# The last 64 keys of two neighbouring batches as one chunk, and the sums of two key chunks in one visit

## The chip, the cores and the metric

The kernel runs on one core of a Trainium2 chip. The core has five engines that work side by side, each with its own queue in order: TensorE (PE, the matrix unit; loads of its stationary operand are shown apart as PEld), VectorE (DVE), ScalarE (ACT), GpSimd (POOL) and SyncE (SP, which issues the DMAs here). SBUF holds tiles of 128 partitions; PE writes into PSUM, 8 banks of 512 float32 per partition. The metric is the device time of one execution in microseconds (us), as the median of several runs.

## The reference

Random-feature attention over 8 batches of 8 heads, 576 positions, 64 values per head, 128 features, then a layer norm and a two-layer MLP with a residual:

```python
def phi(x):
    proj = np.einsum('bhsd,md->bhsm', x, omega)
    sq = np.sum(x * x, axis=-1, keepdims=True) / 2.0
    h = proj - sq
    h = h - np.max(h, axis=-1, keepdims=True)
    return np.exp(h) / np.sqrt(m)
q_p, k_p = (phi(q_s), phi(k_s))
kv = np.einsum('bhsm,bhsd->bhmd', k_p, v)
z = np.sum(k_p, axis=2)
num = np.einsum('bhsm,bhmd->bhsd', q_p, kv)
den = np.einsum('bhsm,bhm->bhs', q_p, z)[..., None] + 1e-06
return (num / den).astype(np.float32)
...
xn = (x - mu) / np.sqrt(var + 1e-06) * g_ln
ch = np.maximum(xn @ w_ch1, 0.0) @ w_ch2
return (x + ch).astype(np.float32)
```

Here x is the attention's output, [batch, position, 8 heads x 64]; w_ch1 is 512 x 2048, w_ch2 2048 x 512.

## The kernel before

**MLP, the stream on PE.** The 8 x 576 = 4608 rows are 9 tiles (t) of 512 rows. For each tile mm1 (L723) computes 16 blocks (f) of 128 hidden features, and mm2 (L759) adds each block into four result banks. Every product is split into three matmuls on high and low parts (L737 to L739, L770 to L772), 3456 in all with 512 columns each. The input xnT is the normalised x, transposed on PE (L710, four 128x128 transposes for each of the 36 row chunks of 128) and split by ACT (L714) and DVE (L716). Weights (w1, w2; 32 loads of 512 KB) are unpacked and split once by ACT and DVE (gen_w, L363 to L434), some ten steps for each.

**Attention.** A batch's 576 keys are five chunks: four of 128 (NFULL) and one of 64 (REM). For each chunk gen_k (L456) loads keys and values (L460, L461), projects the keys (L518, 8 matmuls that the trace shows as 16 records), takes the maximum on DVE (L521) and the exponential on ACT (L527, 8 of them) into a tile kp, and then forms the sums (L491): for each head two matmuls of 64 features x 65 columns (64 values and a one, so that z comes along), 16 matmuls or 32 records. After each chunk of batches 1 to 7 the sums are added into the tile kv by DVE (L504; the first is copied, L507); batch 0's five chunks add up in PSUM instead (banks 6 and 7) and are copied once. The queries go by 36 chunks of 128 rows (gen_q, L535): the first 8 are projected in fp32 (L550), the others in split matmuls (L568, L569); then a copy out of PSUM (L573), a maximum over partitions on POOL (L580), DVE's difference (L585) and ACT's exponential (L588). gen_x (L611) forms numerators and denominators with kv (L627, a visit of 32 records), divides (L634 to L638) and takes the row's statistics (L655, L657).

**What sets the order.** All of this is written by generators, which a planner (class Plan, L68) runs through a model of engines, latencies and free places; the order in which it lets them go on is the order of the program. The steps on PE that interrupt the MLP's stream are called visits below. A part with a lower rank goes first; one that holds PSUM banks is moved ahead by 100 (L57). Once the MLP runs, all visits share one pair of PSUM banks (b_at, banks 0 and 1), mm1 has two banks and mm2 four; before that every pair is free to use, except banks 6 and 7 for batch 0's sums. VISIT (0.37 us) is what the planner adds to a visit's cost. While PE would stand idle in the start, gen_warm (L796) sets in small bf16 matmuls ("spin", L336).

**Places.** "wide" tiles (4) take raw keys and queries and serve weight steps; v (3 places), kp (2), kv (3) and quad (5) serve the attention. In the start, batch 0's loads may also use the weight tiles that are filled last: n_first names them, two for each of FIRST = 4 f (L288). kTr and vR hold the 64-key chunks: kTr is [batch, 128, 4, 64], vR [batch, 64, 8, 65].

Of the kernel before, what the change touches and what calls it, by code (L numbers as in the profile page):

```python
# [16 lines left out]
AF = mybir.ActivationFunctionType  # L17
# [187 lines left out]
def favor_ffn(ctx, tc, kT, kTr, vF, vR, qT, qD, omT, gT, w1, w2, out):  # L205
# [93 lines left out]
    def at_now():  # L299
        return b_at if mlp_on else banks  # L300

    def pairs_now():
        return (b_at,) if mlp_on else tuple(banks[i : i + 2] for i in range(0, 8, 2))

# [131 lines left out]
    kvs, phis, xs, xnTs, pvs, pvt = {}, {}, {}, {}, {}, {}  # L436


    def gen_keys():
        for b in range(B):  # L440
            if b == 1:
                yield wait("w", 2, GATE_K)
            t_kv = yield "get", n_kv
            kvs[b] = t_kv, heads_of(t_kv)
            for c in range(NFULL + 1):
                plan.cur.rank = NS * (b * S // T) + RK + 2 * c
                r = P if c < NFULL else REM
                first = n_first if b == 0 else ()
                k_turn = () if first else ((yield "get", turn["k"]),)
                t_k = yield "get", first + n_big  # L450
                kraw = tile_of(t_k, [P, NP, r])
                t_v = yield "get", first + n_v
                v = heads_of(t_v)
                plan.add(plan.cur.rank, gen_k(b, c, r, kraw, v, (t_k, *k_turn), t_v, n_kp + first))

    def gen_k(b, c, r, kraw, v, early, t_v, n_kp):  # L456
        rank = plan.cur.rank
        kv = kvs[b][1]
        yield dma(2 * P * NP * r)
        nc.sync.dma_start(kraw, kT[b, c] if c < NFULL else kTr[b])  # L460
        nc.sync.dma_start(v[0:r], vF[b, c] if c < NFULL else vR[b])  # L461
        if c:
            yield wait("k", b, c - 1)
        t_kp = yield "get", n_kp
        t_mb = yield "get", n_mb
        late = t_kp, t_mb, t_v
        done(("k", b, c))
        kp = tile_of(late[0], [P, H, M])
        mb = tile_of(late[1], [P, H])
        yield wait("om")  # L470

        def values():
            yield us(DVE, 0.08)
            nc.vector.memset(v[0:r, :, D : D + 1], 1.0)
            done(("v", b, c))

        def sums():
            yield wait("v", b, c)
            yield wait("kp", b, c)
            if c:  # L480
                yield wait("kvmm", b, c - 1)
            if b:
                pvs[0] = yield "pair", pairs_now()
            elif c == 0:
                pvs[0] = banks[6:8]
            t_b = pvs[0]
            yield "run", {PE: VISIT + 0.94}, 0.03
            pv = two(t_b, 4 * (D + 1)).rearrange("p s (a b) -> p s a b", b=D + 1)
            for h in range(H):
                for a in (0, D):  # L490
                    nc.tensor.matmul(  # L491
                        pv[a : a + D, h // 4, h % 4], kp[0:r, slot(h), a : a + D], v[0:r, h],
                        start=(b > 0 or c + h % 4 == 0), stop=(b > 0 or (c == NFULL and h % 4 == 3)),
                    )
            done(("kvmm", b, c))
            free(*late)
            if b == 0 and c < NFULL:
                return
            o = kv.rearrange("p (s a) b -> p s (a b)", s=2)
            pv = two(t_b, 4 * (D + 1))  # L500
            if b and c:
                yield wait("kv", b, c - 1)
                yield dve(8 * (D + 1))
                nc.vector.tensor_tensor(out=o, in0=pv, in1=o, op=ALU.add)  # L504
            else:
                eng = yield "run", {ACT: 0.53, DVE: 0.61}
                copy(eng, o, pv)  # L507
            free(*t_b)
            done(("kv", b, c))

        plan.add(rank, values())
        t_b = yield "pair", pairs_now()
        yield "run", {PE: VISIT + 0.95}, 0.03
        pk = two(t_b).rearrange("p s (a b) -> p s a b", b=M)
        for p in range(NP):
            for h in range(2):
                a = slice(h * D, (h + 1) * D)
                nc.tensor.matmul(pk[0:r, h, p], kraw[a, p], om[a], start=True, stop=True)  # L518
        free(*early)
        yield dve(8 * M)  # L520
        nc.vector.tensor_reduce(  # L521
            out=mb[0:r].rearrange("p (s a) -> p s a", s=2), in_=pk[0:r], axis=AX.X, op=ALU.max, negate=True
        )
        for s in range(2):
            yield us(ACT, 1.0)
            for j in range(4 * s, 4 * s + 4):
                nc.scalar.activation(  # L527
                    out=kp[0:r, j], in_=pk[0:r, s, j % 4], func=AF.Exp, scale=1.0, bias=mb[0:r, j : j + 1]
                )
            free(t_b[s])  # L530
        done(("kp", b, c))
        yield from sums()


    def gen_q(c):  # L535
        first = n_first if c < TC else ()
        q_turn = () if first else ((yield "get", turn["q"]),)
        t_q = yield "get", first + (n_big if c < QF else n_quad)
        if c < QF:
            qraw = tile_of(t_q, [P, 4 * P])  # L540
            yield dma(P * 4 * P)
            nc.sync.dma_start(qraw, qT[c].rearrange("p a b -> p (a b)"))
            yield wait("om")
            free(*q_turn)
            t_b = yield "pair", pairs_now()
            yield "run", {PE: VISIT + 0.92}, 0.03
            pq = two(t_b)
            for h in range(2):
                a = slice(h * D, (h + 1) * D)
                nc.tensor.matmul(pq[:, h], om[a], qraw[a], start=True, stop=True)  # L550
# [29 lines left out]
        nc.gpsimd.partition_all_reduce(  # L580
            mx.rearrange("p a b -> p (a b)"), qc.rearrange("p a b -> p (a b)"), P, bass_isa.ReduceOp.max
        )
# [28 lines left out]
    def gen_x(c, b_turn):  # L611
# [1 line left out]
        parts = [(a, (c * P + a) // S) for a in (0, D)]  # L613
        yield wait("phi", c)
        for b in sorted({b for _, b in parts}):
            yield wait("kv", b, NFULL)
# [6 lines left out]
        yield "run", {PE: VISIT + 0.94}, 0.03  # L623
# [216 lines left out]


LINE = 16
FIRST = 4
N_BIG, N_QUAD = 4, 5
VISIT = 0.37
QF = 2 * TC
# [43 lines left out]
```

## Time and profile before

| | |
|---|---|
| median of 3 runs | 1012.36 us (1011.81 to 1012.91) |
| the profiled execution | 1012.05 us, its span 1010.3 us |
| PE busy | 999.3 us, 99% of the span |
| DVE, ACT, POOL busy | 463.9, 353.4, 120.3 us |
| MLP matmuls (six lines) | 576 each, 390 to 403 ns each |
| first MLP matmul | at 42.06 us |
| DMA | 63.12 MB, mean 62 GB/s |

The span runs from the first to the last instruction that the profile shows. A matmul's duration in the trace is its own, from start to end; matmuls overlap, so what one costs in a row of many is the distance of two starts. A row of the timeline is start, duration, engine, line, operation, output<-input, shape, count, and in brackets the idle time of the engine before it with what ended that. A row of the stages is the stretch, its length, then busy time and instructions of PE, PEld, DVE, ACT and POOL (of PE alone where only PE was asked for), PE's granted clock as a share of full speed, the DMA engines' share and GB/s. A row of groups ends with the busy time, the mean in ns of one, and the idle time before. Line numbers are those of the kernel before; the changed kernel's are given where its order is shown.

### The profile page before, as it was taken

The page shows a single profiled execution, that of the slowest core. Times are in us where ns is not written, and L with a number is a line of the kernel's source. Part 1 is how long each engine was busy: PE and PEld are TensorE (multiplying, and loading weights), DVE is VectorE, ACT ScalarE, POOL GpSimd, SP SyncE. Part 2 cuts the span into 40 slices and gives each one's busy share as a digit, 9 for nine tenths or more (in the row PEclk, how much of TensorE's full clock was granted, in tenths as well). Part 3 has the DMA queues.
Part 4 walks back from the last instruction along what each step waited for, and adds up shares of the span by engine and source line. Part 5 has one row for each costly group of instructions (what it writes and reads, how often), then busy time and mean ns, then how long its engine had stood idle before and what let it go on. Part 6 is the DMA issues. An engine that isn't in the chain of part 4 may idle for free.

```text
span 1010.3 us, 16259 instructions
## 1 busy us (share of the span) xinstructions
PE 999.3 (99%) x6934; PEld 805.3 (80%) x6934; DVE 463.9 (46%) x763; ACT 353.4 (35%) x734; POOL 120.3 (12%) x44
## 2 busy tenths in 40 slices
PE   8999999999999999999999999999999999999998
PEld 6777777787887777887887888888888888888886
DVE  7999964363483343643157323641373143113112
ACT  6788743443443353243124412321232021011110
POOL 5010120220310310121003100320041000000000
PEclk9999999999999999999999999999999999999999
DMA  9346322121131110410032000200110010001001
GB/s 348 126 141 243 125 89 98 34 101 54 32 137 51 52 31 7 168 49 6 1 126 84 12 1 12 94 21 1 55 71 1 1 42 1 1 1 42 1 1 42
DMA packets 26343, 63.12 MB, mean 62 GB/s; under 512 B 3104, under 2 KB 4256, under 8 KB 26272
## 3 DMA queue, kind: packets, MB, share of 16 engines
q1 hardware_dynamic: 26272, 62.09, 17.8%
q8 instruction: 54, 0.88, 0.4%
q14 instruction: 17, 0.14, 0.0%
HBM read 52.64 MB, written 9.44 MB: 61 GB/s over the span
## 4 chain that ended last, share of the span: by engine, by line
PE 92%; DVE 4%; DMA 2%; ACT 1%; issue 0%; SPq 0%; ACTq 0%
PE b L770 14%; PE b L737 13%; PE b L771 12%; PE b L772 12%; PE b L738 12%; PE b L739 12%; PE b L491 4%; PE b L518 4%; PE b L627 3%; PE b L710 2%; PE b L568 1%; PE b L569 1%; DMA w<-w 1%; DVE wide L393 1%; DMA wide<-qT 1%; DVE w L379 1%
## 5 line engine op out<-in xcount | busy, mean ns | idle before, releaser
L750 DVE SCALAR_TENSOR_TENSOR hid<-b,hid 128x512 fp32r<-128x512 f32 x144 | 99.3, 689 | 382.6 <-ACT hid L748 382.4
L748 ACT ACTIVATE hid<-b 128x512 fp32r<-128x512 f32 x144 | 86.3, 600 | 418.6 <-PE b L739 418.2
L770 PE MATMUL b<-w,hid 128*128 128x512 f32 x576 | 231.9, 403 | 0.0
L737 PE MATMUL b<-xnT,w 128*128 128x512 f32 x576 | 229.8, 399 | 0.0
L738 PE MATMUL b<-xnT,w 128*128 128x512 f32 x576 | 224.8, 390 | 0.1
L771 PE MATMUL b<-w,hid 128*128 128x512 f32 x576 | 224.7, 390 | 0.0
L772 PE MATMUL b<-w,hid 128*128 128x512 f32 x576 | 224.6, 390 | 0.0
L739 PE MATMUL b<-xnT,w 128*128 128x512 f32 x576 | 224.4, 390 | 0.0
L580 POOL PARTITION_ALL_REDUCE quad<-quad x34 | 111.2, 3282 | 643.2 <-ACT quad L250 470.6
L770 PEld LDWEIGHTS b<-w,hid 128*128 128x128 f32 x576 | 108.1, 188 | 27.5 <-issue 3.0
L737 PEld LDWEIGHTS b<-xnT,w 128*128 128x128 f32 x576 | 108.0, 188 | 26.2 <-issue 1.3
L772 PEld LDWEIGHTS b<-w,hid 128*128 128x128 f32 x576 | 108.1, 188 | 23.4
L739 PEld LDWEIGHTS b<-xnT,w 128*128 128x128 f32 x576 | 108.1, 188 | 23.3 <-DVE xnT L716 0.3
L738 PEld LDWEIGHTS b<-xnT,w 128*128 128x128 f32 x576 | 108.2, 188 | 21.3 <-DVE w L413 0.5
L771 PEld LDWEIGHTS b<-w,hid 128*128 128x128 f32 x576 | 108.2, 188 | 20.2
L527 ACT ACTIVATE kp<-b,mb 128x128 f32<-128x128 f32 (+1 forms) x296 | 81.6, 380 | 76.2 <-DVE mb L521 76.2
L521 DVE TENSOR_REDUCE mb<-b 128x8 f32<-128x1024 f32 (+1 forms) x40 | 48.6, 1218 | 30.1 <-PE b L518 29.8
L588 ACT ACTIVATE quad<-quad 128x1024 f32<-128x1024 f32 x36 | 38.4, 1068 | 67.6 <-DVE quad L585 67.2
L585 DVE TENSOR_TENSOR quad<-quad,quad 128x1024 f32<-128x1024 f32 x34 | 50.1, 1473 | 23.9 <-POOL quad L580 23.6
L250 ACT COPY quad<-b 128x1024 f32<-128x1024 f32 x30 | 30.4, 1014 | 46.4 <-PE b L569 44.6
L627 PEld LDWEIGHTS b<-kv,quad 128*64 128x64 f32 x1152 | 36.4, 137 | 11.6 <-issue 6.9
L491 PEld LDWEIGHTS b<-v,kp 128*64 128x64 f32 (+1 forms) x1120 | 35.5, 136 | 12.4 <-issue 9.2
(77 smaller groups left out, 745.5 us busy)
## 6 DMA issues: line engine op xcount, KB each, us to landing
w<-w SPq DMA_DIRECT2D x32, 512.0 KB, 6.5
quad<-qD SPq DMA_DIRECT2D x28, 512.0 KB, 3.3
out<-x SPq DMA_DIRECT2D x36, 256.0 KB, 2.0
v<-vF SPq DMA_DIRECT2D x28, 260.0 KB, 3.1
wide<-kT SPq DMA_DIRECT2D x28, 256.0 KB, 3.6
wide<-qT SPq DMA_DIRECT2D x8, 256.0 KB, 3.3
w<-vF SPq DMA_DIRECT2D x4, 260.0 KB, 4.7
v<-vR SPq DMA_DIRECT2D x8, 130.0 KB, 2.5
```

Source lines behind the costliest of these rows:

```text
L491: nc.tensor.matmul(pv[a : a + D, h // 4, h % 4], kp[0:r, slot(h), a : a + D], v[0:r, h], start=(b > 0 or c + h % 4 == 0), stop=(b > 0 or ( ...
L527: nc.scalar.activation(out=kp[0:r, j], in_=pk[0:r, s, j % 4], func=AF.Exp, scale=1.0, bias=mb[0:r, j : j + 1])
L580: nc.gpsimd.partition_all_reduce(mx.rearrange("p a b -> p (a b)"), qc.rearrange("p a b -> p (a b)"), P, bass_isa.ReduceOp.max)
L627: nc.tensor.matmul(pn[a : a + D, h // 4, h % 4], phi[:, h % 2, h // 2, a : a + D], kvs[b][1][:, h], start=True, stop=True,)
L737: nc.tensor.matmul(ph, w[:, 0, cs], xnT[:, 0, k], start=(k == 0), stop=False)
L738: nc.tensor.matmul(ph, w[:, 1, cs], xnT[:, 0, k], start=False, stop=False)
L739: nc.tensor.matmul(ph, w[:, 0, cs], xnT[:, 1, k], start=False, stop=(k == NK - 1))
L748: nc.scalar.activation(out=hl[:, 0], in_=ph, func=AF.Relu)
L750: nc.vector.scalar_tensor_tensor(out=hl[:, 1], in0=ph, scalar=0.0, in1=f32(hl[:, 0]), op0=ALU.max, op1=ALU.subtract)
L770: nc.tensor.matmul(accs[i], hl[:, 0, cs], w[:, 0], start=(f == 0), stop=False)
L771: nc.tensor.matmul(accs[i], hl[:, 0, cs], w[:, 1], start=False, stop=False)
L772: nc.tensor.matmul(accs[i], hl[:, 1, cs], w[:, 0], start=False, stop=(f == NF - 1))
```

## The change

- The 64-key chunks of batches 2i and 2i+1 become one chunk of 128 keys, made with the even batch: one load of keys, one projection, one maximum, one set of exponentials. Its sums are still formed for each batch, over all 128 rows, against a values tile of its own in which the other batch's 64 rows are zero. vR is now [batch, 128, 8, 65] with zeros, kTr [4, 128, 4, 128].
- The sums are a generator of their own, gen_sums, for a group of chunks: [0], [1], [2], [3] for batch 0, [0, 1] and [2, 3] for the others, and the shared chunk alone. A group of two is one visit: for each head the first chunk's two matmuls start the PSUM region and the second chunk's add to it. kv then takes one addition for each group; the first group that is formed is copied.
- An odd batch begins with its share of the shared chunk (g = 0), which is planned along with the even batch's.
- FIRST is 6 in place of 4, so that 12 weight tiles serve the first loads. VISIT is added only once the MLP runs, 0.1 before.

The diff, without lines that only rename, and without gen_k's unchanged steps:

```diff
+    def visit():
+        return VISIT if mlp_on else 0.1
...
     def gen_keys():
+        last = None
         for b in range(B):
             if b == 1:
                 yield wait("w", 2, GATE_K)
-            t_kv = yield "get", n_kv
-            kvs[b] = t_kv, heads_of(t_kv)
-            for c in range(NFULL + 1):
-                plan.cur.rank = NS * (b * S // T) + RK + 2 * c
-                r = P if c < NFULL else REM
+            rank = NS * (b * S // T) + RK
+            groups = [[0], [1], [2], [3]] if b == 0 else [[0, 1], [2, 3]]
+            groups += [] if b % 2 else [[NFULL]]
+            for g, group in enumerate(groups):
+                plan.add(
+                    rank + 2 * group[-1] + 1, gen_sums(b, [(b, c) for c in group], g + b % 2, g == len(groups) - 1)
+                )
+            if b % 2 == 0:
+                plan.add(rank + 2 * NFULL + 1, gen_sums(b + 1, [(b, NFULL)], 0, False))
+            for c in range(NFULL + (b % 2 == 0)):
+                plan.cur.rank = rank + 2 * c
                 first = n_first if b == 0 else ()
                 k_turn = () if first else ((yield "get", turn["k"]),)
                 t_k = yield "get", first + n_big
-                kraw = tile_of(t_k, [P, NP, r])
-                t_v = yield "get", first + n_v
-                v = heads_of(t_v)
+                kraw = tile_of(t_k, [P, NP, P])
+                owners = (b,) if c < NFULL else (b, b + 1)
+                t_v = yield "get", first + n_v, len(owners)
...
-        nc.sync.dma_start(kraw, kT[b, c] if c < NFULL else kTr[b])
-        nc.sync.dma_start(v[0:r], vF[b, c] if c < NFULL else vR[b])
+        nc.sync.dma_start(kraw, kT[b, c] if c < NFULL else kTr[b // 2])
+        vs = []
+        for o, t in zip(owners, t_v):
+            vs.append(heads_of(t))
+            nc.sync.dma_start(vs[-1], vF[o, c] if c < NFULL else vR[o])
...
+    def gen_sums(o, group, g, last):
+        for key in group:
+            yield wait("v", *key)
+            yield wait("kp", *key)
+        if g:
+            yield wait("kvmm", o, g - 1)
+        else:
+            t_kv = yield "get", n_kv
+            kvs[o] = t_kv, heads_of(t_kv)
+        if o:
+            t_b = yield "pair", pairs_now()
+        else:
+            t_b = pvs[0] = banks[6:8]
+        yield "run", {PE: visit() + 0.94 * len(group)}, 0.03
+        pv = two(t_b, 4 * (D + 1)).rearrange("p s (a b) -> p s a b", b=D + 1)
+        for h in range(H):
+            for i, key in enumerate(group):
+                kp, v = kps[key][1], kps[key][2][o][1]
+                for a in (0, D):
+                    nc.tensor.matmul(
+                        pv[a : a + D, h // 4, h % 4], kp[:, slot(h), a : a + D], v[:, h],
+                        start=i == 0 and (o > 0 or g + h % 4 == 0),
+                        stop=i == len(group) - 1 and (o > 0 or (last and h % 4 == 3)),
+                    )
...
+        out = kvs[o][1].rearrange("p (s a) b -> p s (a b)", s=2)
+        pv = two(t_b, 4 * (D + 1))
+        if o and g:
+            yield wait("kv", o, g - 1)
+            yield dve(8 * (D + 1))
+            nc.vector.tensor_tensor(out=out, in0=pv, in1=out, op=ALU.add)
+        else:
+            eng = yield "run", {ACT: 0.53, DVE: 0.61}
+            copy(eng, out, pv)
...
-FIRST = 4
+FIRST = 6
...
+    kTr = k4[..., NFULL * P :].reshape(B // 2, 2, P, NP, REM).transpose(0, 2, 3, 1, 4)
+    kTr = np.ascontiguousarray(kTr).reshape(B // 2, P, NP, P)
...
+    vR = np.zeros((B // 2, 2, 2, REM, H, D + 1), v.dtype)
+    for i in range(2):
+        vR[:, i, i] = pad[i::2, NFULL * P :]
+    vR = vR.reshape(B, P, H, D + 1)
```

gen_sums replaces the inner function sums of gen_k, which did the same for one chunk (L477 to L509 before). gen_x waits for the key "kvall", set when a batch's last group is in kv, in place of its last chunk.

More of the change, by code (lines that the diff above doesn't have):

```diff
@@ L436, in favor_ffn @@
     kvs, phis, xs, xnTs, pvs, pvt = {}, {}, {}, {}, {}, {}
+    kps = {}
     def gen_keys():
+        last = None
         for b in range(B):
@@ new lines, in gen_keys, with gen_k @@
+                owners = (b,) if c < NFULL else (b, b + 1)
+                t_v = yield "get", first + n_v, len(owners)
+                plan.add(plan.cur.rank, gen_k(b, c, kraw, (t_k, *k_turn), owners, t_v, n_kp + first, last))
+                last = b, c
+    def gen_k(b, c, kraw, early, owners, t_v, n_kp, last):
+        rank = plan.cur.rank
+        yield dma(2 * P * NP * P)
+        nc.sync.dma_start(kraw, kT[b, c] if c < NFULL else kTr[b // 2])
[3 more added lines that the diff above has]
+            nc.sync.dma_start(vs[-1], vF[o, c] if c < NFULL else vR[o])
+        if last:
+            yield wait("k", *last)
@@ L464, in gen_k @@
         t_kp = yield "get", n_kp
         t_mb = yield "get", n_mb
-        late = t_kp, t_mb, t_v
         done(("k", b, c))
-        kp = tile_of(late[0], [P, H, M])
-        mb = tile_of(late[1], [P, H])
+        kp = tile_of(t_kp, [P, H, M])
+        mb = tile_of(t_mb, [P, H])
+        kps[b, c] = [t_kp, kp, dict(zip(owners, zip(t_v, vs))), len(owners)]
         yield wait("om")
         def values():
-            yield us(DVE, 0.08)
-            nc.vector.memset(v[0:r, :, D : D + 1], 1.0)
+            yield us(DVE, 0.08 * len(owners))
+            for o, v in zip(owners, vs):
+                rows = slice(0, P) if c < NFULL else slice(o % 2 * D, o % 2 * D + D)
+                nc.vector.memset(v[rows, :, D : D + 1], 1.0)
@@ L475, in values @@
             done(("v", b, c))
[L477 to L509, printed above, removed]
@@ L511, in gen_k @@
         plan.add(rank, values())
         t_b = yield "pair", pairs_now()
-        yield "run", {PE: VISIT + 0.95}, 0.03
+        yield "run", {PE: visit() + 0.95}, 0.03
         pk = two(t_b).rearrange("p s (a b) -> p s a b", b=M)
@@ L517, in gen_k @@
                 a = slice(h * D, (h + 1) * D)
-                nc.tensor.matmul(pk[0:r, h, p], kraw[a, p], om[a], start=True, stop=True)
+                nc.tensor.matmul(pk[:, h, p], kraw[a, p], om[a], start=True, stop=True)
         free(*early)
@@ L521, in gen_k @@
         nc.vector.tensor_reduce(
-            out=mb[0:r].rearrange("p (s a) -> p s a", s=2), in_=pk[0:r], axis=AX.X, op=ALU.max, negate=True
+            out=mb.rearrange("p (s a) -> p s a", s=2), in_=pk, axis=AX.X, op=ALU.max, negate=True
         )
@@ L527, in gen_k @@
                 nc.scalar.activation(
-                    out=kp[0:r, j], in_=pk[0:r, s, j % 4], func=AF.Exp, scale=1.0, bias=mb[0:r, j : j + 1]
+                    out=kp[:, j], in_=pk[:, s, j % 4], func=AF.Exp, scale=1.0, bias=mb[:, j : j + 1]
                 )
             free(t_b[s])
+        free(t_mb)
         done(("kp", b, c))
-        yield from sums()
+    def gen_sums(o, group, g, last):
[22 more added lines that the diff above has]
+                    )
+        for key in group:
+            free(kps[key][2][o][0])
+            kps[key][3] -= 1
+            if not kps[key][3]:
+                free(kps[key][0])
+        done(("kvmm", o, g))
+        if o == 0 and not last:
+            return
+        out = kvs[o][1].rearrange("p (s a) b -> p s (a b)", s=2)
[7 more added lines that the diff above has]
+            copy(eng, out, pv)
+        free(*t_b)
+        done(("kv", o, g))
+        if last:
+            done(("kvall", o))
     def gen_q(c):
@@ L545, in gen_q @@
             t_b = yield "pair", pairs_now()
-            yield "run", {PE: VISIT + 0.92}, 0.03
+            yield "run", {PE: visit() + 0.92}, 0.03
             pq = two(t_b)
@@ L615, in gen_x @@
         for b in sorted({b for _, b in parts}):
-            yield wait("kv", b, NFULL)
+            yield wait("kvall", b)
         t_x = yield "get", n_x
@@ L622, in gen_x @@
         t_b = yield "pair", pairs_now()
-        yield "run", {PE: VISIT + 0.94}, 0.03
+        yield "run", {PE: visit() + 0.94}, 0.03
         pn = two(t_b, 4 * (D + 1)).rearrange("p s (a b) -> p s a b", b=D + 1)
@@ L857 @@
     kT = np.ascontiguousarray(k4[..., : NFULL * P].reshape(B, P, NP, NFULL, P).transpose(0, 3, 1, 2, 4))
-    kTr = np.ascontiguousarray(k4[..., NFULL * P :])
+    kTr = k4[..., NFULL * P :].reshape(B // 2, 2, P, NP, REM).transpose(0, 2, 3, 1, 4)
+    kTr = np.ascontiguousarray(kTr).reshape(B // 2, P, NP, P)
     pad = np.zeros((B, S, H, D + 1), v.dtype)
```

7 lines of the change are left out of this document (removed).

## The prediction

> **What bounds the kernel now.** I read the page first: its head, the busy times and the chain that ended last.
>
> ```profile
> span 1010.3 us, 16259 instructions
> PE 999.3 (99%) x6934; PEld 805.3 (80%) x6934; DVE 463.9 (46%) x763; ACT 353.4 (35%) x734; POOL 120.3 (12%) x44
> PE 92%; DVE 4%; DMA 2%; ACT 1%; issue 0%; SPq 0%; ACTq 0%
> ```
>
> PE is busy all the time and is 92% of the chain. The 8% that isn't PE lies in the start and the tail. So two things can shorten the run: less time on PE once the MLP's stream runs, and an earlier start of that stream. Next comes PE's timeline, at a spot without and at two with attention work (columns: start, duration, instruction), and the stages, which give PE's busy time and, in brackets, its instructions.
>
> ```profile
> 44.30:55.64 11.34, 11.34 (x51) 1.00 0.00 0
> 163.74 0.39 PE L739 MATMUL b<-xnT,w 128*128 128x512 f32 x1
> 164.06 1.16 PE L518 MATMUL b<-om,wide 64*128 64x128 f32 x16
> 165.15 0.50 PE L737 MATMUL b<-xnT,w 128*128 128x512 f32 x1
> 165.49 0.39 PE L738 MATMUL b<-xnT,w 128*128 128x512 f32 x1
> ...
> 169.82 0.39 PE L739 MATMUL b<-xnT,w 128*128 128x512 f32 x1
> 170.14 1.16 PE L491 MATMUL b<-v,kp 128*64 128x65 f32 x32
> 171.22 0.50 PE L737 MATMUL b<-xnT,w 128*128 128x512 f32 x1
> 171.56 0.40 PE L738 MATMUL b<-xnT,w 128*128 128x512 f32 x1
> 171.80 0.39 PE L739 MATMUL b<-xnT,w 128*128 128x512 f32 x1
> 172.03 0.40 PE L737 MATMUL b<-xnT,w 128*128 128x512 f32 x1
> 172.26 0.39 PE L738 MATMUL b<-xnT,w 128*128 128x512 f32 x1
> 172.49 0.39 PE L739 MATMUL b<-xnT,w 128*128 128x512 f32 x1
> ```
>
> In the undisturbed stretch 50 MLP matmuls start in 11.34 us (the 51st instruction only reaches into it): 0.227 us a step. The sums' visit reads so: the step before it takes 0.32 us (169.82 to 170.14), the visit 1.08, the step after it 0.34, the next four 0.23 each. From 169.82 to 172.49 is 2.67 us; six steps of 0.227 are 1.36, so the visit costs 1.31: **1.08 of work and 0.23 of entering and leaving**. The projection's visit likewise: 1.09 of work (164.06 to 165.15), the same 0.32 and 0.34, so 1.32.
>
> **The change part by part.** *(1) Four projections fewer.* The 64-key chunks are what goes: seven in the stream before, three 128-key chunks in their place now (the eighth, batch 0's, lies in the start in both).
>
> ```profile
> 109.12 1.09 PE L518 MATMUL b<-om,wide 64*64 64x128 f32 x16
> 110.14 0.50 PE L770 MATMUL b<-w,hid 128*128 128x512 f32 x1
> ...
> L518 PEld LDWEIGHTS b<-om,wide 64*128 64x128 f32 x448 | 27.2, 187 | 11.1 <-issue 8.2 <-DVE quad L252 1.3 <-ACT quad L250 0.5
> L518 PEld LDWEIGHTS b<-om,wide 64*64 64x64 f32 x128 | 6.8, 132 | 2.6 <-issue 2.1 <-DVE wide L393 0.4
> ```
>
> A 64-key projection works 1.02 us (109.12 to 110.14) against 1.09 for 128 keys, so half the keys cost nearly the whole visit. Saved: 7 x (1.02 + 0.23) - 3 x 1.32 = **4.8 us**. The Trainium skill speaks against this: "TensorE: Matmul & The Clock Gate", LDWEIGHTS, says that a weight load's time goes with its columns, 64 or 128 here. Were the visit bound by that, a 64-key one would work some 0.55 us and the saving would be 7 x 0.78 - 3 x 1.32 = 1.5 us. The rows don't follow it: the load takes 132 ns against 187, and the visit hardly shortens; I go by the visit.
>
> *(2) Sums.* Padding gives the last chunk's sums 128 rows for 64, twice (once for each batch), so their number stays. These groups of the sums, by shape, show that rows are free: 221 ns at 64 rows, 224 at 128.
>
> ```profile
> L491 PE MATMUL b<-v,kp 128*64 128x65 f32 x896 | 32.3, 224 | 0.0
> L491 PE MATMUL b<-v,kp 64*64 64x65 f32 x224 | 8.1, 221 | 0.0
> ```
>
> What changes is how they are cut into visits. PE's order in batch 1, before: two neighbouring chunks' sums (v is the values' tile, kp the keys' features), with six MLP matmuls between.
>
> ```order
> 430 L491 MATMUL b<-v_838,kp_854 64x65 x16
> 431 L770 MATMUL b<-w_60_1009,hid_998 128x512
> 432 L771 MATMUL b<-w_60_1009,hid_998 128x512
> 433 L772 MATMUL b<-w_60_1009,hid_998 128x512
> 434 L770 MATMUL b<-w_60_1009,hid_998 128x512
> 435 L771 MATMUL b<-w_60_1009,hid_998 128x512
> 436 L772 MATMUL b<-w_60_1009,hid_998 128x512
> 437 L491 MATMUL b<-v_924,kp_951 64x65 x16
> ```
>
> Now, for the same batch's last pair of chunks:
>
> ```order
> 536 L802 MATMUL b<-w_80_1158,hid_1241 128x512
> 537 L537 MATMUL b<-v_1049,kp_1127 64x65 x2
> 538 L537 MATMUL b<-v_1142,kp_1144 64x65 x2
> 539 L537 MATMUL b<-v_1049,kp_1127 64x65 x2
> 540 L537 MATMUL b<-v_1142,kp_1144 64x65 x2
> ```
>
> The two chunks alternate head by head, 32 matmuls on end, and the stream resumes in row 553. Over the whole order 35 sums' visits in the stream become 14 double and 6 single ones; the 35th (batch 1's share of the first pair's chunk) moves into the start. Before: 35 x 1.31 = 45.9 us. Now: 14 x (2 x 1.08 + 0.23) + 6 x 1.31 = 41.3. Saved: **4.5 us**, of which 1.3 is the move.
>
> The trace has no fp32 matmul of 65 columns that adds to what its predecessor just wrote from another chunk, as each double visit's second chunk does. Bounds: nothing (each of these matmuls is two records, which go into the same columns without a visible gap: 32 records in 1.08 us), or a wait for the predecessor's whole 222 ns at each of 8 heads. I take nothing; the other end is a rival.
>
> *(3) Transposes.* The planner sets them into the stream differently: a run of them that stands alone occurs 9 times before, 15 times now; their number is the same. Leaving one costs a step of 0.32 for 0.227:
>
> ```profile
> 275.89 1.18 PE L710 MATMUL b<-ident,wide 128*128 128x128 f32 x8
> 276.82 0.48 PE L770 MATMUL b<-w,hid 128*128 128x512 f32 x1
> 277.14 0.39 PE L771 MATMUL b<-w,hid 128*128 128x512 f32 x1
> ```
>
> Six more cost 6 x 0.09 = **0.6 us**. The projections of queries (4) and the numerators (32 visits) stay. The stream is thus shorter by 4.8 + 4.5 - 0.6 = **8.7 us**.
>
> *(4) Off PE.* Of the 28 adds of this row 14 go, and four of the 40 maxima with their 32 exponentials; nobody on PE waits for them now, so they are worth nothing by themselves.
>
> ```profile
> L504 DVE TENSOR_TENSOR kv<-b,kv 128x520 f32<-128x520 f32 x28 | 19.5, 696 | 53.1 <-PE b L491 53.1
> 539.50 1.16 PE L518 MATMUL b<-om,wide 64*128 64x128 f32 x16 [0.89 <-DVE quad L252]
> ```
>
> The second row is the largest stall that PE has in the stream: the projection waits 0.89 us for the one pair of PSUM banks that all visits share, since DVE copies a query projection late. Fewer visits use that pair now, but the order is a new one: I expect such a stall to go or to come back elsewhere, and credit 0.4.
>
> *(5) The start.* What holds it now, in the rows of each engine:
>
> ```profile
> 0.00:20.00 20.00, 16.11 (x204) 11.56 (x206) 14.05 (x17) 12.38 (x33) 10.44 (x9) 1.00 0.91 331
> 18.20 1.13 PE L550 MATMUL b<-wide,om 64*128 64x512 f32 x4 [0.67 <-DMA wide<-qT]
> 15.38 3.43 POOL L580 PARTITION_ALL_REDUCE w<-quad  x1
> 21.92 3.74 POOL L580 PARTITION_ALL_REDUCE w<-quad  x1 [3.11 <-ACT quad L250]
> 26.59 0.59 ACT L250 COPY kv<-b 128x520 f32<-128x520 f32 x1 [0.24 <-PE b L336]
> 30.91 0.68 DVE L638 TENSOR_TENSOR x<-b,dn 128x512 f32<-128x512 f32 x1
> 41.90 0.68 DVE L716 TENSOR_TENSOR xnT<-b,xnT 128x512 fp32r<-128x512 f32 x1
> 42.06 0.48 PE L737 MATMUL b<-xnT,w 128*128 128x512 f32 x1
> 42.64 0.50 PE L739 MATMUL b<-xnT,w 128*128 128x512 f32 x1
> ```
>
> The fourth query tile comes late (18.20, a DMA), so POOL stands idle 3.11 us before its last maximum. The stream starts at 42.06, but its third matmul waits for the last xnT on DVE (41.90 + 0.68) and goes at 42.64. SP's queue before, from the third query load on:
>
> ```order
> 11 L542 DMA wide_99<-qT 128x512
> 12 L460 DMA w_120_93<-kT 128x512
> 13 L461 DMA w_120_94<-vF 128x520
> 14 L460 DMA wide_95<-kTr 128x256
> 15 L461 DMA v_96<-vR 64x520
> 16 L368 DMA w_00_151<-w 128x1024
> 17 L368 DMA w_00_158<-w 128x1024
> 18 L368 DMA w_10_161<-w 128x1024
> 19 L542 DMA wide_155<-qT 128x512
> ```
>
> And now:
>
> ```order
> 11 L572 DMA wide_93<-qT 128x512
> 12 L473 DMA w_120_89<-kT 128x512
> 13 L477 DMA w_120_135<-vF 128x520
> 14 L572 DMA wide_94<-qT 128x512
> 15 L473 DMA w_110_90<-kTr 128x512
> 16 L477 DMA w_110_154<-vR 128x520
> 17 L477 DMA w_100_156<-vR 128x520
> 18 L371 DMA w_00_158<-w 128x1024
> ```
>
> The fourth query load has moved ahead of the weights, so POOL's last maximum can follow the third (15.38 + 3.43 = 18.8), some 3 us sooner. Against that the first weight load stands behind 0.78 MB more (0.26 of it the moved queries, 0.13 keys, 0.39 values): at 331 GB/s 2.4 us later. Then keys and values of batch 1 add work just where batch 0's sums end; DVE's order, before and now, up to the first attention output x:
>
> ```order
> 27 L634 TENSOR_SCALAR dn_410<-b 128x8
> 28 L432 TENSOR_TENSOR w_00_445<-wide_286,w_00_445 128x512
> 29 L636 RECIPROCAL dn_410<-dn_410 128x8
> 30 L413 SCALAR_TENSOR_TENSOR w_00_440<-wide_264,g_sb,w_00_440 128x128 x4
> 31 L638 TENSOR_TENSOR x_409<-b,dn_410 128x512
> ```
>
> ```order
> 19 L615 TENSOR_TENSOR w_150_266<-w_150_266,w_120_291 128x1024
> 20 L388 TENSOR_SCALAR wide_422<-w_00_172 128x512
> 21 L252 COPY kv_369<-b 128x520
> 22 L382 SCALAR_TENSOR_TENSOR w_00_158<-w_00_158,wide_404 128x512
> ```
>
> Batch 1's kv copy (some 0.6 us, by ACT's row) stands in front of x, and its sums (1.08 on PE) go in front of batch 0's by the planner's order. So kv of batch 0 comes about when it did (26.6: the sooner queries against 1.08 us). Over the whole start DVE has less to do, as steps moved behind the last xnT or to ACT. What such steps take, from one start to the next:
>
> ```profile
> 10.88 1.20 DVE L252 COPY quad<-b 128x1024 f32<-128x1024 f32 x1
> 28.14 0.68 DVE L379 SCALAR_TENSOR_TENSOR w<-w,wide 128x512 uint32<-128x512 uint32 x1
> 28.74 0.41 DVE L252 CAST w<-wide 128x512 fp32r<-128x512 f32 x1
> 40.00:60.00 20.00, 19.92 (x97) 16.05 (x96) 20.00 (x42) 18.20 (x38) 0.00 (x0) 1.00 0.00 1
> ```
>
> Up to the last xnT the order has three sign merges (L379) fewer, 0.6 each, and one 128x1024 copy fewer, 1.2; against that about 1.5 us more of other weight steps and the kv copy. Net 1.5 us less on the engine that ends the start. The ends: 3 us sooner (POOL's whole gap), 2 us later (the weights' delay shows, or the two kv steps). I take **1.0 us sooner**, nearer to DVE's sum.
>
> Sum against the profiled execution: 8.7 + 0.4 + 1.0 = 10.1 us. That execution took 1012.05 us, 1.75 outside its span, 0.3 under the median of 1012.36, from which I count: **1002.3 us**.
>
> **The rivals.** *A: the start gives nothing or loses.* If the weights' 2.4 us or batch 1's steps come last, the stream starts up to 2 us later than at 42.06: 1012.4 - 9.1 + 2 = 1005.3. For it: DVE (the third engine in the last row) works 20 us of 20 from 40 to 60 us, so it has no slack to make good a late weight. Against: by then nearly all of the first weights lie in SBUF, and between the last xnT and the last step of the fourth weight DVE's order has no more rows than before.
>
> *B: new stalls in the stream.* Both kp tiles are held till the double visit, and the next keys' projection waits for one; queries and sums meet in the one bank pair in a new order. Three or four stalls like the 0.89 us above give 3 us: 1012.4 - 9.7 + 3 = 1005.7. Against: PE stands idle 11 us in all (1010.3 - 999.3), start and tail included, and outside the transposes the order leaves at least six MLP matmuls between two visits, as before.
>
> *C: the second chunk waits in PSUM (slower).* If each matmul that adds into columns just written waits for its predecessor's end, 8 heads in 14 visits lose about 0.22 - 0.07 us for each of the two column halves in turn: 112 x 0.15 = 17 us, and the run takes 1012.4 - 10.1 + 17 = 1019. It turns slower once a head loses over 10.1 / 112 = 0.09 us. Against: MLP matmuls add to one bank every 0.227 us while each lasts 0.39, overlapped.
>
> *D: visits merge only in name*: PE is charged by chunk, not by visit, so the 14 x 0.23 = 3.2 us stay: 1005.5. Against: the excess lies in the two steps at the visit's edges.
>
> **How the numbers follow.** Forecast 0.70, A 0.12, B 0.10, C 0.03, D 0.05. The forecast's own terms move by -2 and +2 in the start and +-0.5 in the stalls: 999.8 to 1004.8; A, B and D reach to 1005.7. Range 999.8 to 1005.8, all but C and the tails of A and B. A run of this kernel can tell about 0.2%, 2 us, from no change: faster 0.95, same 0.02, slower 0.03.
>
> **What would show it.** In the new trace: sums' groups of 64 matmul records taking 2.16 us between MLP steps of 0.32 and 0.34 (longer: C); 31 projections in the stream at 1.09; stream's steps undisturbed at 0.227; POOL without its gap before the fourth maximum; the third MLP matmul near 41.6. A stream start after 43, or PE's idle time above 3 us behind it, would make the prediction wrong.

## The result and the profile after

The changed kernel took 1001.66, 1000.82 and 1001.21 us, median 1001.21, against 1012.28 for the kernel before on the same chip: a ratio of 0.9891 [0.9871, 0.991]. A fourth run took 1985.69 us, for a reason that no record shows, and isn't counted. The forecast was 1002.3 us. The profiled execution took 1001.66 us, 10.39 less than that of before.

The head of the page after, its busy times and the chain that ended last:

```profile
span 999.9 us, 16072 instructions
PE 991.8 (99%) x6888; PEld 804.7 (80%) x6888; DVE 448.8 (45%) x749; ACT 343.7 (34%) x698; POOL 121.3 (12%) x44
PE 90%; DVE 5%; ACT 2%; DMA 2%; POOL 1%; issue 1%; SPq 0%; POOLq 0%; ACTq 0%; DVEq 0%
```

PE is 99% busy as before, with 7.5 us less to do (999.3 to 991.8); the other 2.9 us of the shorter span are idle time of PE (11.0 before, 8.1 now). Now PE's timeline at a double visit, the answer to the two single visits shown of before:

```profile
83.63 0.39 PE L769 MATMUL b<-xnT,w 128*128 128x512 f32 x1
83.95 2.09 PE L537 MATMUL b<-v,kp 128*64 128x65 f32 x64
85.96 0.50 PE L767 MATMUL b<-xnT,w 128*128 128x512 f32 x1
86.30 0.39 PE L768 MATMUL b<-xnT,w 128*128 128x512 f32 x1
```

The edges are what they were, 0.32 before and 0.34 behind. The work from start to start is 2.01 us, not twice 1.08: **two chunks in one visit save 0.15 of work besides the 0.23 at the edges**. So 0.14 to 0.15 of a visit's 1.08 is paid once for a visit; it is called the tail below, though where in the visit it lies isn't shown. The groups on PE that changed (31 projections of 16 records from wide tiles, 34 shares of 32 records):

```profile
L502 PE MATMUL b<-om,wide 64*128 64x128 f32 x496 | 36.5, 285 | 0.9 <-ACT quad L250 0.6 <-DVE x L668 0.4
L537 PE MATMUL b<-v,kp 128*64 128x65 f32 x1088 | 36.1, 223 | 0.0
```

Where PE waits in the stream, in its timeline after:

```profile
71.30 1.16 PE L502 MATMUL b<-om,wide 64*128 64x128 f32 x16 [0.59 <-ACT quad L250]
77.42 1.61 PE L502 MATMUL b<-om,wide 64*128 64x128 f32 x16
430.35 1.15 PE L657 MATMUL b<-kv,quad 128*64 128x65 f32 x32 [0.46 <-DVE quad L252]
543.35 1.16 PE L502 MATMUL b<-om,wide 64*128 64x128 f32 x16 [0.36 <-DVE x L668]
```

The 0.89 us stall of before is gone, and three of 0.36 to 0.59 stand in its place; a fourth hides in the visit at 77.42, which takes 1.61 for 1.16. Last, the start, from the timelines of POOL, DVE, ACT and PE:

```profile
5.50 1.77 PE L502 MATMUL b<-om,w 64*128 64x128 f32 x16
18.82 3.30 POOL L610 PARTITION_ALL_REDUCE w<-w  x1
26.02 0.59 ACT L250 COPY kv<-b 128x520 f32<-128x520 f32 x1
30.11 0.68 DVE L668 TENSOR_TENSOR x<-b,dn 128x512 f32<-128x512 f32 x1
35.68 0.68 DVE L746 TENSOR_TENSOR xnT<-b,xnT 128x512 fp32r<-128x512 f32 x1
42.10 0.68 DVE L746 TENSOR_TENSOR xnT<-b,xnT 128x512 fp32r<-128x512 f32 x1
42.43 0.47 PE L767 MATMUL b<-xnT,w 128*128 128x512 f32 x1
42.97 0.39 PE L769 MATMUL b<-xnT,w 128*128 128x512 f32 x1
```

POOL's gap is closed and its last maximum comes 3.1 us sooner (18.82 for 21.92), kv 0.6 sooner (26.02 for 26.59), x 0.8 sooner. But the last xnT and the stream come later: 42.43 for 42.06.

Added up over PE's whole timeline, profile against profile: the start loses 0.4 us; the stream, from its first MLP matmul to the start of PE's last instruction, shrinks from 964.0 to 953.3, by 10.7. Of these the sums give 6.2 (visits with their edges: 44.9 to 38.7), the projections 4.6 by their count, the transposes 0.3, and small irregular steps of the MLP 0.5; the waits take back 0.8 (1.3 to 2.1, that at 77.42 included).

### The profile page after: what moved, and what is told of

It reads as the page before. It is cut to its first block, busy times and chain, and to the rows that moved or that the text cites. A ratio compares the mean times of both kernels' runs of the same rounds, so it can differ in the third digit from the quotient of the medians.

```text
span 999.9 us, 16072 instructions
## 1 busy us (share of the span) xinstructions
PE 991.8 (99%) x6888; PEld 804.7 (80%) x6888; DVE 448.8 (45%) x749; ACT 343.7 (34%) x698; POOL 121.3 (12%) x44
## 4 chain that ended last, share of the span: by engine, by line
PE 90%; DVE 5%; ACT 2%; DMA 2%; POOL 1%; issue 1%; SPq 0%; POOLq 0%; ACTq 0%; DVEq 0%
PE b L800 13%; PE b L767 13%; PE b L802 12%; PE b L801 12%; PE b L769 12%; PE b L768 12%; PE b L657 4%; PE b L502 3%; PE b L537 3%; PE b L740 1%; PE b L598 1%; PE b L599 1%; POOL quad L610 1%; DVE w L382 1%; DMA w<-w 1%
## 5 line engine op out<-in xcount | busy, mean ns | idle before, releaser
L511 ACT ACTIVATE kp<-b,mb 128x128 f32<-128x128 f32 x264 | 74.3, 387 | 63.6 <-DVE mb L505 49.2
L505 DVE TENSOR_REDUCE mb<-b 128x8 f32<-128x1024 f32 x36 | 43.9, 1220 | 38.9 <-PE b L502 38.5
L615 DVE TENSOR_TENSOR quad<-quad,quad 128x1024 f32<-128x1024 f32 x34 | 47.4, 1394 | 18.2 <-POOL quad L610 18.0
L250 ACT COPY quad<-b 128x1024 f32<-128x1024 f32 x33 | 33.4, 1013 | 52.2 <-PE b L599 42.8
L657 PE MATMUL b<-kv,quad 128*64 128x65 f32 x1120 | 39.9, 224 | 0.5 <-DVE quad L252 0.5
```

What stands on the lines that cost most here:

```text
L511: nc.scalar.activation(out=kp[:, j], in_=pk[:, s, j % 4], func=AF.Exp, scale=1.0, bias=mb[:, j : j + 1])
L657: nc.tensor.matmul(pn[a : a + D, h // 4, h % 4], phi[:, h % 2, h // 2, a : a + D], kvs[b][1][:, h], start=True, stop=True,)
```

## Experiments

The theory after the result: fewer visits, each worth its edges and its tail, are the gain; the second chunk's accumulation costs nothing; the start gives little. "After" is the changed kernel; each ratio is to the kernel before, run beside that experiment.

**1. No pairs, shared chunk kept.** Does a merge save anything, and how much?

```diff
-            groups = [[0], [1], [2], [3]] if b == 0 else [[0, 1], [2, 3]]
+            groups = [[0], [1], [2], [3]] if True else [[0, 1], [2, 3]]
```

> The changed kernel with every key chunk's sums in a visit of its own again; the shared 64-key chunks stay. Theory (a visit's entry and exit are paid on PE for each visit, and the double visits of the changed kernel took 2.02 us against 1.08 for a single one): 14 more visits, each 2 x 1.08 - 2.02 + 0.23 = 0.37 us, 5.2 us in all, so 1001.4 + 5.2 = 1006.6. Rival (only the edges' steps of 0.32 and 0.34 count, the shorter double visit is an artefact of the records): 14 x 0.23 = 3.2, so 1004.6. Rival (PE is charged by chunk): 1001.4. The stream's start is as in the changed kernel by both, within 0.5 us.

Measured: 1008.61 us (1007.56 to 1011.25), ratio 0.9962 [0.9949, 0.9976]. Without the one disturbed visit below, visits and edges of the sums take about 5 us more than after (14 merges at 0.37 make 5.2). So rival D falls: the merge is real. The two executions whose clock reads 1.00 took 1007.56 and 1008.01, still some 1.2 us above the 1006.6 expected; no profile shows why. The profiled one (1011.25) lies 4.6 above it; the timelines of DVE and PE show where:

```profile
431.48 2.92 DVE L615 TENSOR_TENSOR quad<-quad,quad 128x1024 f32<-128x1024 f32 x1 [3.09 <-POOL quad L610]
437.79 2.00 PE L537 MATMUL b<-v,kp 128*64 128x65 f32 x32 [2.62 <-DVE x L668]
440.31 0.63 PE L768 MATMUL b<-xnT,w 128*128 128x512 f32 x1
440.74 0.63 PE L769 MATMUL b<-xnT,w 128*128 128x512 f32 x1
```

and the stages (the row as the prediction's are read, with the granted clock behind POOL's column):

```profile
437.70:443.00 5.30, 5.21 (x42) 4.06 (x44) 3.90 (x7) 1.99 (x2) 0.00 (x0) 0.50 0.17 54
```

A sums' visit waits 2.62 us for the one bank pair, which x (L668) reads late. Ahead of x DVE's difference on the queries (L615) took 2.92 us, where after's 34 take 1.39 on average; what made it long isn't settled. Then PE runs at half its clock (0.50 in the row, steps of 0.43 us for 0.227). By the trace's clock records, from which the stages' clock is worked out, it does so from 437.16 to 443.99 us, 6.83 us. The Trainium skill, "TensorE: Matmul & The Clock Gate", Part 1, says that PE's clock falls to half after an idle window of about 3.4 us and rises after a busy one. The row agrees with the halving; the idle time here was shorter, 2.62 us.

**2. Pairs kept, 64-key chunks apart again.** What is the shared chunk worth?

```diff
-            groups += [] if b % 2 else [[NFULL]]
+            groups += [[NFULL]]
...
-            for c in range(NFULL + (b % 2 == 0)):
+            for c in range(NFULL + 1):
...
-        nc.sync.dma_start(kraw, kT[b, c] if c < NFULL else kTr[b // 2])
+        nc.sync.dma_start(kraw, kT[b, c] if c < NFULL else kTr[b])
...
-                        pv[a : a + D, h // 4, h % 4], kp[:, slot(h), a : a + D], v[:, h],
+                        pv[a : a + D, h // 4, h % 4], kp[0:r, slot(h), a : a + D], v[0:r, h],
```

> The changed kernel with the 64-key chunks of each batch loaded, projected and summed apart again (as before the change); the double visits and FIRST = 6 stay. Theory (a 64-key projection costs PE nearly what a 128-key one does): seven projections of 1.02 + 0.23 in place of three of 1.32 give 4.8 us, and batch 1's 64 keys have their sums in the stream and not in the start, 1.3 us: 1001.4 + 6.1 = 1007.5, less what the start gains without batch 1's share, up to 1 us. Rival (a projection goes with its keys): 1.5 + 1.3, so 1004.2. In the profile: 64-key projections of 1.02 us.

Measured: 1008.57 us (1008.14 to 1009.65), ratio 0.9961 [0.9948, 0.9973]. The stream is 6.4 us longer than after's, where the step from the visits' length gave 6.1, so a 64-key projection does cost nearly a whole visit. The start gains nothing without batch 1's share, where up to 1 us was expected (table in experiment 7). The rule of the Trainium skill ("TensorE: Matmul & The Clock Gate", LDWEIGHTS), taken as the length of a visit, would have put this kernel at 1004.2; the measurement decides against that reading.

**3. Chunk by chunk instead of head by head.** Does adding to what was just written cost a wait (rival C)? Here the second chunk's matmul comes 16 matmuls after the one it adds to.

```diff
-        for h in range(H):
-            for i, key in enumerate(group):
-                kp, v = kps[key][1], kps[key][2][o][1]
+        for i, key in enumerate(group):
+            kp, v = kps[key][1], kps[key][2][o][1]
+            for h in range(H):
...
-                        start=i == 0 and (o > 0 or g + h % 4 == 0),
-                        stop=i == len(group) - 1 and (o > 0 or (last and h % 4 == 3)),
+                        start=i + h % 4 == 0 and (o > 0 or g == 0),
+                        stop=i == len(group) - 1 and h % 4 == 3 and (o > 0 or last),
```

> The changed kernel, with the matmuls of a double visit chunk by chunk (all heads of the first chunk, then all of the second) in place of head by head, so that no matmul adds to columns that the one or two before it wrote. Theory (adding to columns just written costs nothing): double visits of 2.02 us as in the changed kernel, 1001.4 +- 0.5. Rival (it costs something): double visits shorter than 2.02, and 14 times the difference off the time.

Measured: 1001.55 us (1001.06 to 1001.85), ratio 0.989 [0.9876, 0.9903]. PE's timeline:

```profile
83.51 0.39 PE L769 MATMUL b<-xnT,w 128*128 128x512 f32 x1
83.83 2.09 PE L537 MATMUL b<-v,kp 128*64 128x65 f32 x64
85.84 0.50 PE L767 MATMUL b<-xnT,w 128*128 128x512 f32 x1
```

2.01 us as in after. Both the length of the visit and the time are the same: rival C falls.

**4. FIRST = 4 in the changed kernel.** What do the more places bring?

```diff
-FIRST = 6
+FIRST = 4
```

> The changed kernel with FIRST = 4, the places for the first loads as before. Theory (the start gained nothing from the change, and the places move only loads): the stream starts within 1 us of 42.4, 1001.4 +- 1. Rival (the places are what keeps the start from becoming longer with 128-key chunk and the two values tiles): the fourth queries' load waits for a place again, the stream starts 2 us later, 1003.4.

Measured: 1002.33 us (1002.04 to 1002.41), ratio 0.9897 [0.9884, 0.9911], 0.6 us (by the ratios) to 1.1 (by the medians) above after. Both the theory and the rival are off: the stream starts at 42.12, but PE's early pace was a fast one, and at equal pace that is 0.7 us late (table in experiment 7), a third of what the rival said. Besides, PE waits once more, for a weight, 15 us into the stream:

```profile
56.82 0.50 PE L768 MATMUL b<-xnT,w 128*128 128x512 f32 x1 [0.57 <-DVE w L416]
```

**5. FIRST = 6 in the kernel before.** The same edit alone, the other way round.

```diff
-FIRST = 4
+FIRST = 6
```

> The kernel before with FIRST = 6 alone: 12 weight tiles as places for the first loads. Theory (the places only move the fourth queries' load ahead of the weights; POOL's gap before its last maximum closes, yet DVE's work still sets when the stream can run): 1012.4 +- 1. Rival (the late query load held the start): 2 to 3 us faster, 1010.

Measured: 1012.7 us (1012.24 to 1013.3), ratio 1.0005 [0.9996, 1.0014]: no difference. More places are worth about 1 us beside the other edits, and nothing by themselves; the rival, which had them as the cause of 2 to 3 us, falls.

**6. Batch 1's share after batch 0's sums.** What does the share that moved into the start cost there?

```diff
     def gen_sums(o, group, g, last):
+        if o == 1 and not g:
+            yield wait("kvmm", 0, NFULL)
```

> The changed kernel with batch 1's share of the first shared chunk held back in the start until batch 0's sums are done, so that batch 0's kv comes 1.08 us sooner. Theory (DVE's work ends the start and feeds PE until the fourth weight, so a sooner stream start comes back as a wait there): the numerators start about 1 us sooner, the stream starts by 42.4 or up to 1 us sooner, and PE waits as much longer for the fourth w1 weight near 56 us: 1001.4 +- 0.7. Rival (the chain through kv and xnT sets the end): 1000.4.

Measured: 999.33 us (999.21 to 999.76), ratio 0.9873 [0.9858, 0.9888]: about 2 us faster than after. The rival has the direction: the chain through kv bears on the start, and the share stood in it. The wait that the theory named came too, but it takes back only 0.4 us; PE's timeline:

```profile
55.81 0.50 PE L770 MATMUL b<-xnT,w 128*128 128x512 f32 x1 [0.39 <-DVE w L416]
```

Some 0.5 of the 2 us lies not in the start but in the stream, which is shorter by that much: the stalls that after has at 77.42 and 543.35 are gone.

**7. The same kernel again.** PE's pace in the first 7 us differs between executions of one kernel. Does it shift the start? One more execution each of after, before and experiment 6.

> The changed kernel once more. Theory (PE's pace in the first 7 us changes between executions of one kernel and the whole start follows it one to one): the fourth-batch-free rule start = (first query projection's start) + 35.33 us holds again, as in the four profiles with this start so far (7.10 and 42.43, 7.24 and 42.56, 6.97 and 42.30, 6.90 and 42.33). Rival (the change itself makes the first projection late): 7 us and 42.4 again. A first query projection near 6.1 would settle it for the theory, with a stream start near 41.4.

> The kernel before once more. Theory (pace of the execution): the first query projection may start anywhere from 5.8 to 7.2 us, and the stream starts 36.0 us after it (6.08 and 42.06 in the first profile). Rival (the kernel before starts early by itself): 6.1 and 42.1 again.

> The changed kernel with batch 1's share held back in the start, once more. Its first profile had the earliest first query projection of all (5.86) and a stream start of 41.08, 35.22 later. Theory (holding the share back gains little, the pace of that execution did it): 35.2 us after the first query projection again. Rival (it shortens the start by 1 us whatever the pace): a stream start of 41.4 or sooner also when the first query projection comes at 7.

(The "rule" of the first of these expectations is only: stream start = start of the first query projection + 35.33 us.) Measured: 1000.81, 1011.95 and 999.72 us. The timeline of after, second execution, PE's and DVE's rows:

```profile
5.24 1.16 PE L502 MATMUL b<-om,w 64*128 64x128 f32 x16
34.81 0.68 DVE L746 TENSOR_TENSOR xnT<-b,xnT 128x512 fp32r<-128x512 f32 x1
41.23 0.68 DVE L746 TENSOR_TENSOR xnT<-b,xnT 128x512 fp32r<-128x512 f32 x1
41.56 0.47 PE L767 MATMUL b<-xnT,w 128*128 128x512 f32 x1
```

The same first projection takes 1.16 here and 1.77 in the first profile, and everything behind it comes 0.87 us sooner, down to the stream (41.56 for 42.43): the theory holds, with 35.33 again. What the pace is, the trace's clock records show: they begin, at full clock, at 6.80 us in the first profile and at 4.91 in the second, and PE's steps fall from 0.21 us to 0.11 at just these times. Ahead of them PE thus runs at half its pace (the stages read a clock of 1.00 there only for want of a record). So at an equal early pace the change starts the stream 0.4 to 0.5 us sooner than before (42.06 and, second execution, 41.93). For the kernel before my expectation failed: its stream came 35.64 us after its query projection, not 36.0; it follows the first key projection instead. The first query projection and the stream's start, from PE's timelines of the changed kernel and its variants:

| profile | query projection | stream | distance |
|---|---|---|---|
| after, first and second execution | 7.10, 6.23 | 42.43, 41.56 | 35.33, 35.33 |
| experiments 1, 3, 9 | 7.24, 6.97, 6.90 | 42.56, 42.30, 42.33 | 35.32, 35.33, 35.43 |
| experiment 2 (64-key chunks apart) | 6.59 | 42.50 | 35.91 |
| experiment 4 (FIRST = 4) | 6.08 | 42.12 | 36.04 |
| experiment 6 (share held back), twice | 5.86, 7.11 | 41.08, 40.99 | 35.22, 33.88 |
| experiment 10 (the same, and more) | 6.21 | 40.09 | 33.88 |
| experiment 8 (weight step held back) | 6.75 | 41.74 | 34.99 |

For experiment 6 the rival holds, and by more than it said: at equal pace its start is 35.33 - 33.88 = 1.45 us shorter, in its second execution and in experiment 10, whose start has the same edit. Its first execution is the exception. PE's timelines, the first execution, the second, and experiment 10:

```profile
30.49 1.13 PE L339 MATMUL b<-spin 128*128 128x252 bf16 x9 [1.26 <-issue]
41.08 0.47 PE L769 MATMUL b<-xnT,w 128*128 128x512 f32 x1
```

```profile
30.41 1.13 PE L339 MATMUL b<-spin 128*128 128x252 bf16 x9 [0.46 <-issue]
40.99 0.48 PE L769 MATMUL b<-xnT,w 128*128 128x512 f32 x1
```

```profile
29.49 1.13 PE L339 MATMUL b<-spin 128*128 128x252 bf16 x9 [0.44 <-issue]
40.09 0.48 PE L769 MATMUL b<-xnT,w 128*128 128x512 f32 x1
```

In the first of them PE stands 1.26 us at a spin, with no wait that the profile names ("issue"), against 0.44 to 0.46 in the other two; what held it isn't shown. Another 0.5 us it had lost by the numerators. From that spin to the stream it is 10.6 us in all three. Fewer spins were not tried.

**8. A weight step held back.** Do DVE's weight steps, taken together, bind (then it comes back as a wait at 56 us), or only those between the xnT pieces?

```diff
+            if f == 1:
+                yield wait("xnT", 0, TC - 1)
             yield "run", {DVE: 0.84}, "two"
```

> The changed kernel, with DVE's 1.05 us low-part step of the second w1 weight put behind the last xnT (the planner fills part of its place with a 0.34 us step). Theory (DVE's sum of work until the fourth weight binds, not the chain to the last xnT): the stream starts 0.5 to 1 us sooner, PE waits about as much more near 56 us, 1001.4 +- 0.5. Rival (the end of the xnT chain sets the time): 1000.6.

Measured: 1000.15 us (999.93 to 1000.59), ratio 0.9881 [0.9864, 0.9897], 1.1 under after, and no new wait at 56 us. The theory that DVE's sum of weight work binds falls. But the rival gets little of the step's 1.05 us: the last xnT now waits for ACT, and at equal pace the stream starts only 0.34 us sooner (34.99 for 35.33 in the table). Most of the rest lies in the stream, which is 0.6 shorter than after's:

```profile
41.56 0.69 DVE L748 TENSOR_TENSOR xnT<-b,xnT 128x512 fp32r<-128x512 f32 x1 [0.32 <-ACT xnT L746]
41.74 0.48 PE L769 MATMUL b<-xnT,w 128*128 128x512 f32 x1
```

**9. Three chunks in one visit.** Does the next merge give the same again? Even batches form [0, 1] and [2, 3, shared]; kp gets 3 places, v 4, quad 4 for 5.

```diff
-            groups = [[0], [1], [2], [3]] if b == 0 else [[0, 1], [2, 3]]
-            groups += [] if b % 2 else [[NFULL]]
+            groups = [[0], [1], [2], [3]] if b == 0 else [[0, 1], [2, 3]] if b % 2 else [[0, 1], [2, 3, NFULL]]
+            groups += [] if b else [[NFULL]]
```

> The changed kernel with one more step the same way: in batches 2, 4 and 6 the shared chunk's sums join the visit of chunks 2 and 3 (three places for kp, four for v, paid for with one quad tile less). Theory (0.37 us for each visit that is merged away): 3 x 0.37 = 1.1 us off, 1000.3, less if the queries' chain now waits for a quad tile. Rival (only the edges' steps count): 3 x 0.23 = 0.7, 1000.7. In the profile: three visits of 96 records of about 2.96 us.

Measured: 998.78 us (997.95 to 999.02), ratio 0.9866 [0.9851, 0.988], 2.4 under after where 1.1 was expected. PE's timeline:

```profile
181.57 0.39 PE L802 MATMUL b<-w,hid 128*128 128x512 f32 x1
181.89 3.02 PE L537 MATMUL b<-v,kp 128*64 128x65 f32 x96
184.84 0.50 PE L800 MATMUL b<-w,hid 128*128 128x512 f32 x1
```

2.95 us for three shares (1.08, 2.01, 2.95): each further share adds 0.93 to 0.94. Three merges at 0.37 give the 1.1. About 0.7 of the rest are stalls: those of after at 430.35 (0.10 us of it is left, at 427.84) and 543.35 are gone, those at 71 and 77 us stay. Whether the places or the order removed them was not tried.

**10. Experiments 6 and 9 together.**

> The two steps that gained by themselves together: batch 1's share held back in the start (2.1 us under the changed kernel when alone) and the shared chunk's sums in the visit of chunks 2 and 3 for batches 2, 4 and 6 (2.7 us when alone). If they lie in different places (start and stream) they add up: 1001.4 - 4.7 = 996.7. If each owes about 1 us to the order that the planner happened on or to PE's slow first microseconds in one profile, 998.

Measured: 997.65 us (997.15 to 998.21), ratio 0.9857 [0.9841, 0.9873]. Added up, the two gains give 996.9; 0.8 of that is lost, and in the stream: the start keeps its 1.45 us, while the stream is 0.4 longer than experiment 9's, where experiment 6 alone made it 0.5 shorter. This is the best version found, 1.4% faster than before.

## Why the prediction was right, point by point

**Projections (1)**: 4.8 said, 4.6 found, and experiment 2 undoes it at the size said.

**Sums (2)**: 4.5 said, 6.2 found. The mechanism held (experiments 1 and 3, and rivals C and D fell with them); the size was off in one place. The double visit was priced at 2 x 1.08 us from the rows of single ones, and 1.08 includes a tail of 0.14 that a merged visit pays once: 14 x 0.14 = 2.0 more. The trace of before had a row that shows it, three visits' numerators on end in the start, of the same shape:

```profile
27.86 3.03 PE L627 MATMUL b<-kv,quad 128*64 128x65 f32 x96
30.82 0.28 PE L336 MATMUL b<-spin 128*128 128x252 bf16 x1
```

From start to start they take 2.96 us, not 3 x 1.08 = 3.24. The edges, 0.20 on average before and not 0.23 (some visits touch transposes), take 0.3 of it back.

**Transposes (3)**: 0.6 lost was said, 0.3 gained found. Their edges do cost 0.4 more, but their own work is 0.8 less (13.7 to 12.9 us). PE's timelines show why: a run of 16 transposes takes 1.70 us (in one case 1.98), a run of 8 takes 0.79 and a run of 4 takes 0.355. Shorter runs thus work less for each transpose, about as much as the exit that each adds; before there were six runs of 16, now there are four.

**Stalls (4)**: 0.4 gained was said, 0.8 lost found. The big one went, as said; four small ones came. Rival B had the right direction and a quarter of its price.

**The start (5)**: 1.0 us sooner was said; the profiled execution shows 0.4 later, and at equal early pace it is 0.4 to 0.5 sooner, so rival A falls too. POOL's gap closed and the weights were not late, as the sum assumed. The step that failed is "net 1.5 us less on the engine that ends the start": DVE's work up to the last xnT was added up, as if DVE were busy throughout. It isn't. Early on its maxima wait for PE. DVE's waits up to 42 us (total, times, longest), first before, then after, where 0.9 us of the total is the slow early pace (3.0 in the second execution):

```profile
DVE mb L521 <- PE b L518: 1.4, 1, 1.4
```

```profile
DVE mb L505 <- PE b L502: 3.9, 4, 2.5
```

And late, DVE's sum isn't what the chain follows. In the second execution the first xnT comes at 34.81, against this row of before, 2.6 us sooner:

```profile
37.44 0.67 DVE L716 TENSOR_TENSOR xnT<-b,xnT 128x512 fp32r<-128x512 f32 x1
```

From there to the last piece it was 4.5 us before (37.44 to 41.90) and is 6.4 now (34.81 to 41.23), so that 2.0 of the 2.6 us were given back. DVE does have 1.8 us more of weight steps between the pieces (4.3 for 2.5), but the trace shows little held up by them: ACT's last cast ends at 41.01, and the weight step ahead of the last piece holds that piece back 0.2 us. Experiment 8 agrees, with 0.34. What comes later is ACT's cast of each piece. ACT's rows, before and then after, second execution (L695 and L725 normalise, L714 and L744 cast):

```profile
36.92 1.33 ACT L695 ACTIVATE wide<-x,st 128x512 f32<-128x512 f32 x2 [0.34 <-DVE st L657]
38.88 0.58 ACT L714 CAST xnT<-b 128x512 fp32r<-128x512 f32 x1 [0.63 <-PE b L710]
39.99 0.58 ACT L714 CAST xnT<-b 128x512 fp32r<-128x512 f32 x1
41.03 0.59 ACT L714 CAST xnT<-b 128x512 fp32r<-128x512 f32 x1
```

```profile
36.22 0.59 ACT L744 CAST xnT<-b 128x512 fp32r<-128x512 f32 x1 [1.57 <-PE b L740]
36.71 0.72 ACT L725 ACTIVATE wide<-x,st 128x512 f32<-128x512 f32 x1
38.18 0.59 ACT L744 CAST xnT<-b 128x512 fp32r<-128x512 f32 x1 [0.18 <-PE b L740]
40.45 0.56 ACT L744 CAST xnT<-b 128x512 fp32r<-128x512 f32 x1
```

Before, ACT normalised two pieces on end, and the last casts came 1.1 and 1.0 us apart. Now it casts a piece, normalises the next, and waits for PE to transpose that before the next cast: 2.0 and 2.3 us apart, 2.1 more in all, about the time given back. A forecast of the start had to follow this order on ACT and PE. This is read from the rows: that another order on ACT wins the time back was not tried, and why the planner chose this one isn't shown.

The errors in the terms (-0.2, +1.7, +0.9, -1.2, -1.4 us against the profile, with 0.5 from small steps that no term had) nearly cancel: the sum said 10.1 us, the profiles show 10.4. That the total came out better than its parts is luck.

## What to carry to other kernels

A short visit to a busy engine costs its two edges and its tail besides its work (here 0.23 and 0.14 of 1.31 us), so merging visits pays even if the number of instructions stays, and the surest price of a visit of double length is a row of such length, not twice a short one. For a start, add up the chain that ends it, piece by piece and across the engines that hand the pieces on; the sum of one engine's work doesn't give the end where that engine also waits, or only fills its time. Before a fraction of a microsecond in the start is put down to an edit, look at a second execution of the same kernel.

## What the runs showed of the hardware that was not expected

- PE's pace in the first microseconds differs between executions of one kernel: the first projection took 1.77 us in one execution of after and 1.16 in the next, and the stream's start followed by 0.87 us. It changes, from steps of 0.21 us to 0.11, where the trace's records of full clock begin: at 6.80 and 4.91 us. The Trainium skill, "TensorE: Matmul & The Clock Gate", Part 1, has a window that runs free of the kernel's start, which would let the faster pace begin at another moment each time. That agrees, and the records show the window's length: their stretches of full or half clock, up to the last matmul, are whole multiples of 3.413 us (2, 126 and 166 in experiment 1, 291 in both executions of after, 295 in that of before).
- An idle time of 2.62 us in mid-stream brought 6.83 us at half clock (experiment 1), which began when PE had been idle for 2.0 us; idle times of up to 1.6 us, in the other profiles after the full clock had begun, brought none.
- At one place in the start PE stood with no wait that the profile names, 0.44 and 0.46 us in two executions and 1.26 in a third with the same edit (experiment 7). That third one lost its early pace, so a single profile of it misleads.
